# Decay exponents of sixteen attention units as a TensorE product, narrower products for Y, and a new order of the first 850 steps

## The chip, the cores and the metric

One core of a Trainium2 chip runs the kernel. The metric is device time in microseconds, taken over whole executions; one further execution is recorded by the hardware profiler, and all rows shown come from that one. Engines: PE is TensorE, DVE is VectorE, ACT is ScalarE, POOL is GpSimd, and SP issues transfers.

## The reference

An mLSTM runs over 4 x 8 heads (B x H) of 768 steps with head size 40, and its output passes through two pairs of dense layers (320 to 2048 to 320):

```python
for t in range(S):
    m_new = np.maximum(f_gate[:, :, t] + m, i_gate[:, :, t])
    f_stab = np.exp(f_gate[:, :, t] + m - m_new)
    i_stab = np.exp(i_gate[:, :, t] - m_new)
    C = f_stab[...] * C + i_stab[...] * np.einsum('bhd,bhe->bhde', vt, kt)
    n = f_stab[...] * n + i_stab[...] * kt
    y[:, :, t] = sigmoid(o_gate) * (C @ qt) / np.maximum(np.abs(n @ qt), 1.0)
h = x @ w_in;  x = (h * np.clip(h + 3.0, 0.0, 6.0) / 6.0) @ w_out     # phase 0
h = x @ w_in2; x = np.maximum(h, 0.0) ** 2 @ w_out2                   # phase 1
```

## The kernel before

**Attention.** The sequence is cut into 12 chunks of 64 steps. A *unit* u is one batch b and one chunk c with all eight heads, so there are 48. For each unit the kernel builds W = exp(G[l] + bT[j]), the decay between a row j and a step l, with G a running sum of gate values and bT a value per row, and rows after the step masked. W has 104 partitions: 64 rows of the chunk and 40 rows (from partition 64, `E0`) for the state carried from the chunk before. The steps of one unit, with their functions: `at_load` (q, k and v; L275), `at_gload` (G read back from DRAM and broadcast to 104 partitions; L287), `w_add` (adds bT; L295), `w_mask` (on POOL; L304), `w_e` (Exp on ACT; L310), `x_q` (q times W for the state rows; L326), `x_k` (k times W's last column; L333), `at_S` (the products of k and q on PE; L355), `at_P` (those times W, on DVE; L384), `at_Y` (the products with v and the state, on PE; L398), `at_C` (the new state), `at_n1` to `at_n3` (the normalization; L415 to L444). For eight units (value "p" in the table `ENG`, L174) `x_q` does nothing: `at_S` passes q through PSUM by a product with an identity (L366), and one `at_P` covers all 104 rows. Units from 22 on (`US`) round q and k to fp32r first (`qk_split`, L346).

**at_Y.** For each head there are two fp32 products: 64 output rows (L404) and 40 output rows (L406). An fp32 product is two records in the trace, so a unit has 32.

**Dense layers.** X is kept as six blocks of 128 steps by four batches. `t_pe`, `t_hi` and `t_lo` (L520 to L539) transpose a block and split it into two fp32r parts. A *slot* s is one block and 128 of the 2048 hidden columns: `mm_A` (eight products, L545), `act1` (ACT, L556), `act1b` (DVE, L564), `act2` (a rounded copy, L572), `act2b` (what is left of it, on DVE, L577), and `mm_B` (three products for each 128 rows, L582). There are 200 slots; the first 16 are of half width (256 columns), the rest of 512. Slots 0 to 23 are block 0, and phase 1 begins with slot 104. Weights come as 64-bit numbers and are decoded by `w_exp` (ACT), `w_b1` and `w_b2` (DVE), `w_hi` (ACT) and `w_lo` (mostly POOL), L484 to L513.

**Order.** Every engine runs its instructions in the order of one list of steps. The first part is written out by hand (`FIRST`, L31 to L101, 704 steps up to slot 30 and unit 21); the rest comes from `moe()` (L649), which places attention steps, transposes and weight steps at slots by hooks (L670 to L703). All transfers are issued by SP. PSUM has eight banks: four accumulators, two (`ps_a`) that `mm_A` uses in turn, one (`ps_s`) for S and transposes, one (`ps_y`) for Y.

Of the kernel before, what the change touches and what calls it, by code (L numbers as in the profile page):

```python
# [43 lines left out]
x_q:4 w_add:5 w_mask:5 w_add:7 gate_b:1 at_S:5 at_P:4,1 at_P:4,0 w_exp:0,4 w_e:6 x_q:6 w_b1:0,4
act1:0 act1:1 w_e:5 at_C:3 w_hi:0,3 x_k:5 w_lo:0,3 x_k:6 w_mask:7 x_q:5 act1b:0 mm_A:2 at_Y:4
act1b:1 w_b2:0,4 at_P:5,0 act2:0 act2:1 w_exp:0,5 act2b:0 at_P:5,1 at_n1:4 at_S:6
mm_A:3 w_b1:0,5 at_n2:4 w_load:0,8 at_load:7 at_P:6,1 w_b2:0,5 act2b:1 w_hi:0,4 act1:2
act1b:2 w_exp:0,6 at_C:4 act1:3 w_e:7 at_n3:4 w_hi:0,5 act2:2 w_lo:0,4 x_k:7 x_q:7 gate_bT:1
at_P:6,0 mm_B:0,1 at_Y:5 at_n1:5 w_b1:0,6 at_gload:8 at_load:8 w_lo:0,5 act2b:2 w_b2:0,6
w_exp:0,7 w_b1:0,7 act1b:3 at_S:7 mm_A:4 at_C:5 w_exp:0,8 at_n2:5 mm_B:1,1 mm_B:2,1  # L50
act1:4 at_P:7,0 at_P:7,1 at_Y:6 w_load:0,11 w_add:8 w_mask:8 at_gload:9 w_load:0,10 w_load:0,9
at_gload:10 at_load:9 at_load:10 at_gload:11 w_b2:0,7 act1b:4 mm_B:0,0 w_hi:0,6 at_C:6 act2:3
w_e:8 at_n1:6 at_S:8 at_P:8,1 mm_B:1,0 w_exp:0,9 w_exp:0,10 w_add:9 w_lo:0,6 w_mask:9
w_e:9 at_n2:6 w_load:0,14 warm o_load:3 load_gates:1 at_P:8,0 at_n3:6 x_k:8 at_n3:5 mm_B:2,0
at_Y:7 w_b1:0,8 act2b:3 at_n1:7 act2:4 act2b:4 w_b2:0,8 w_hi:0,7 t_pe:0,0,2 t_hi:0,0,2
# [721 lines left out]
```

## Time and profile before

| what | value |
|---|---|
| median of 3 runs | 871.29 us (871.28 to 873.6) |
| the profiled execution | 871.86 us |
| span in its profile | 870.1 us, 15963 instructions |
| mean granted TensorE clock | 0.99 of full speed |

The span runs from the first to the last instruction of the program; 1.76 us of the profiled execution lie around it. Busy times come from records: those of PE are pipelined and their ends are modelled, so distances between starts are the better measure there. Idle time in front of an instruction is put down to the event that ended it.

### The profile page before, as it was taken

The page shows a single profiled execution, that of the slowest core. Times are in us where ns is not written, and L with a number is a line of the kernel's source. Part 1 is how long each engine was busy: PE and PEld are TensorE (multiplying, and loading weights), DVE is VectorE, ACT ScalarE, POOL GpSimd, SP SyncE. Part 2 cuts the span into 40 slices and gives each one's busy share as a digit, 9 for nine tenths or more (in the row PEclk, how much of TensorE's full clock was granted, in tenths as well). Part 3 has the DMA queues.
Part 4 walks back from the last instruction along what each step waited for, and adds up shares of the span by engine and source line. Part 5 has one row for each costly group of instructions (what it writes and reads, how often), then busy time and mean ns, then how long its engine had stood idle before and what let it go on. Part 6 is the DMA issues. An engine that isn't in the chain of part 4 may idle for free.

```text
span 870.1 us, 15963 instructions
## 1 busy us (share of the span) xinstructions
PE 825.9 (95%) x6288; PEld 738.0 (85%) x6288; DVE 559.5 (64%) x938; ACT 427.4 (49%) x817; POOL 260.7 (30%) x240
## 2 busy tenths in 40 slices
...
GB/s 222 269 232 134 169 81 36 92 100 96 170 92 97 103 86 108 95 81 82 1 3 167 201 163 1 1 31 1 1 31 1 20 12 1 31 1 1 31 1 31
DMA packets 30694, 66.82 MB, mean 77 GB/s; under 512 B 5116, under 2 KB 17468, under 8 KB 30620
## 3 DMA queue, kind: packets, MB, share of 16 engines
...
q14 instruction: 25, 0.20, 0.1%
...
## 4 chain that ended last, share of the span: by engine, by line
PE 73%; DVE 16%; issue 5%; ACT 3%; POOL 1%; DMA 1%; SPq 0%; DVEq 0%; POOLq 0%; ACTq 0%
PE hps L551 33%; PE acc L590 32%; DVE wt L492 4%; DVE gl L580 3%; PE Yp L404 3%; PE Sp L372 2%; DVE g L567 2%; PE tp L525 2%; DVE wt L498 1%; DVE X L444 1%; ACT yt L431 1%; ACT g L560 1%; DVE gh L575 1%; DVE Xm L395 1%; PE Sp L379 1%
## 5 line engine op out<-in xcount | busy, mean ns | idle before, releaser
L551 PE MATMUL hps<-xs,wi 128*128 128x512 f32 (+1 forms) x1600 | 392.6, 389 | 4.2 <-DVE g L567 2.4
L590 PE MATMUL acc<-wo,gh 128*128 128x320 f32 x1536 | 349.5, 314 | 0.3 <-ACT X L597 0.3
L551 PEld LDWEIGHTS hps<-xs,wi 128*128 128x128 f32 x1600 | 290.5, 193 | 53.5 <-DVE g L567 2.7
L590 PEld LDWEIGHTS acc<-wo,gh 128*128 128x128 f32 x1536 | 259.6, 189 | 9.9 <-ACT X L597 0.5
L590 PE MATMUL acc<-wo,gl 128*128 128x320 f32 x768 | 239.3, 312 | 5.0 <-DVE gl L580 5.0
L580 DVE TENSOR_TENSOR gl<-g,gh 128x512 fp32r<-128x512 f32 (+1 forms) x200 | 154.2, 771 | 61.7 <-ACT gh L575 60.6
L575 ACT CAST gh<-g 128x512 fp32r<-128x512 f32 (+1 forms) x192 | 115.1, 600 | 75.3 <-DVE g L570 58.7
L570 DVE TENSOR_TENSOR g<-g 128x512 f32<-128x512 f32 x96 | 66.4, 692 | 133.2 <-ACT g L562 133.2
L590 PEld LDWEIGHTS acc<-wo,gl 128*128 128x128 f32 x768 | 144.9, 189 | 7.6 <-DVE gl L580 7.5
L560 ACT ACTIVATE g<-hps,three 128x512 f32<-128x512 f32 (+1 forms) x104 | 67.8, 655 | 152.0 <-PE hps L551 138.4
L562 ACT ACTIVATE g<-hps 128x512 f32<-128x512 f32 x96 | 57.3, 597 | 143.4 <-PE hps L551 143.4
L567 DVE SCALAR_TENSOR_TENSOR g<-g,hps 128x512 f32<-128x512 f32 (+1 forms) x104 | 66.8, 644 | 65.0 <-ACT g L560 64.5
L329 POOL TENSOR_TENSOR Xm<-qkt,W 40x512 f32<-40x512 f32 x36 | 49.8, 1384 | 119.2 <-ACT W L319 113.6
L404 PEld LDWEIGHTS Yp<-Z,Xm 104*64 104x64 f32 x768 | 54.5, 151 | 21.8 <-issue 13.3
L404 PE MATMUL Yp<-Z,Xm 104*64 104x41 f32 x768 | 60.6, 244 | 8.8 <-DVE Xm L388 3.8
L300 POOL TENSOR_TENSOR W<-W,bT 104x512 f32<-104x512 f32 x43 | 59.4, 1382 | 3.4 <-DMA W<-Gd 3.0
L406 PE MATMUL Yp<-Z,Xm 104*40 104x41 f32 x768 | 52.7, 225 | 0.3 <-POOL Xm L340 0.3
L512 POOL TENSOR_TENSOR wi<-wt,wi 128x768 fp32r<-128x768 f32 x14 | 27.6, 1970 | 83.7 <-ACT wi L507 83.5
L340 POOL TENSOR_TENSOR Xm<-kI,W 104x320 f32<-104x320 f32 x43 | 40.5, 944 | 25.2 <-DMA Z<-in_va 10.4
L406 PEld LDWEIGHTS Yp<-Z,Xm 104*40 104x40 f32 x768 | 46.5, 123 | 0.4 <-POOL Xm L340 0.4
L351 DVE SCALAR_TENSOR_TENSOR qs<-qs,less,qkt 120x512 fp32r<-120x512 f32 x52 | 37.6, 764 | 7.5 <-ACT qs L349 7.3
L306 POOL TENSOR_SCALAR_AFFINE_SELECT W<-W 64x512 f32<-64x512 f32 x48 | 36.7, 767 | 9.7 <-DVE W L300 6.8
...
## 6 DMA issues: line engine op xcount, KB each, us to landing
...
W<-Gd SPq DMA_DIRECT2D x48, 208.0 KB
...
```

The costliest lines, as they stand in the source:

```text
L300: on("w_add", "g", u).tensor_tensor(out=W, in0=W, in1=bT[:, c, b * H:(b + 1) * H].unsqueeze(2).to_broadcast([KX, H, L]), op=ALU.add)
L329: on("x_q", "g", u).tensor_tensor(out=x_tile(u)[E0:KX, :, 0:L], in0=T["qk", u][E0:KX, 0], in1=T["W", u][E0:KX], op=ALU.mult)
L404: nc.tensor.matmul(out=Yp[0:L, h, :], lhsT=Xm[:, h, 0:L], rhs=Z[b][c % 2][:, h, :], start=True, stop=True)
L406: nc.tensor.matmul(out=Yp[E0:KX, h, :], lhsT=Xm[:, h, L:KX], rhs=Z[b][c % 2][:, h, :], start=True, stop=True)
L551: nc.tensor.matmul(out=h, lhsT=w[:, hl, kk, o:o + P], rhs=t[:, xk, i0 * P:i1 * P], start=(i == 0), stop=(i == len(TERMS) - 1))
L560: nc.scalar.activation(out=g, in_=T["h", s], func=ACTF.Relu, bias=three)
L562: nc.scalar.activation(out=g, in_=T["h", s], func=ACTF.Relu)
L567: nc.vector.scalar_tensor_tensor(out=g, in0=g, scalar=6.0, in1=T["h", s], op0=ALU.min, op1=ALU.mult)
L570: nc.vector.tensor_tensor(out=g, in0=g, in1=g, op=ALU.mult)
L575: copy("act2", s)(out=gh, in_=g)
L580: nc.vector.tensor_tensor(out=gl, in0=g, in1=gh.bitcast(F32), op=ALU.subtract)
L590: nc.tensor.matmul(out=acc[i], lhsT=g[:, n], rhs=w[:, hl, m % MG, :], start=(m == 0 and q == 0), stop=(m == NM - 1 and q == 2))
```

## The change

- For the first 16 units (`U1`) W's exponent is made on PE (`w_pe`): one bf16 product of an identity with a mask, then one fp32r product of `gb` (the row values bT as a rounded part and its remainder, and two rows of ones) with `R[b]` (rows that select the heads, and two rows that hold G's rounded part and remainder). `w_e` reads the sum from PSUM. `w_add` and `w_mask` are left out for these units. G goes to `R[b]` by two small transfers inside the core, issued by ACT, not by a broadcast from DRAM. The bank is that of an accumulator for units 0 to 7, and `ps_s` for 8 to 15.
- The same 16 units send q through PSUM in `at_S` (eight did so before).
- In all units `at_Y` computes each head in four products with at most 32 output rows (32, 32, 32, 8), where there were two.
- In slots 0 to 23 `act1b` writes g over h in its PSUM bank, so that `act2` and `act2b` read PSUM.
- The constants are made in five smaller steps, with eight ACT copies for the head rows (`head_rows`); two gate steps move from POOL to DVE.
- The written list is new: 845 steps, up to slot 40 and unit 26. A mark "@v", "@g" or "@a" names the engine in place of the table `ENG`. Before `mm_A:30` both lists have the steps of 30 slots, all 16 weight tiles of phase 0 and `at_Y` of 20 units.
- Phase 1's weight decoding starts a tile every one and a half slots, where it was every slot.

```diff
@@ -29,75 +30,86 @@
 FIRST = """
-o_load:1 load_gates:0 o_load:0 o_sig:0 o_sig:1 at_load:0 at_load:1 const_init gate_m:0 gate_g:0
-gate_G:0 gate_b:0 gate_bT:0 gate_m:1 gate_g:1 at_load:2 at_gload:0 at_gload:1 w_load:0,0
-at_gload:2 at_gload:3 w_add:0 w_mask:0 w_e:0 x_q:0 w_add:1 w_mask:1 at_S:0 at_S:1 at_S:2
...
-t_pe:0,0,0 at_C:2 w_add:6 t_hi:0,0,0 t_lo:0,0,0 warm at_n3:3 w_exp:0,3 t_pe:0,0,1 warm w_hi:0,2
-t_hi:0,0,1 w_b1:0,3 w_b2:0,3 t_lo:0,0,1 w_lo:0,2 mm_A:0 at_S:4 mm_A:1 x_k:4 w_mask:6
...
+const_g load_gates:0 const_z:0 const_i at_load:0 head_rows:1 at_load:1 const_z:1 head_rows:0
+const_l const_z:3 const_z:2 head_rows:2 gate_m:0 o_load:0 const_k:1 at_load:2 gate_g:0 head_rows:3
+at_S:0 gate_G:0 w_load:0,0 gate_b:0 at_gload:0 at_gload:4 at_gload:1 const_k:2 gate_bT:0 at_S:1
+at_gload:5 const_k:0 w_load:0,2 gate_m:1 gate_g:1 w_pe:0 gate_G:1 o_sig:0 w_pe:1 gate_b:1 w_e:0
+w_load:0,1 w_e:1 at_P:0,0 x_k:0 at_gload:2 at_P:1,0 at_gload:3 gate_bT:1 at_Y:0 x_k:1@v at_S:2
...
+t_lo:0,0,1 w_exp:0,3 w_lo:0,2@v mm_A:0 w_load:0,7 w_b2:0,1 mm_A:1 act1:0 w_b1:0,4 w_hi:0,1 at_S:4
...
+at_P:5,0 at_Y:4 w_exp:0,5 at_load:8 w_lo:0,4 act1b:3 mm_B:0,0 act2:2 at_n1:4 at_S:6 at_C:4 act2b:2
+load_gates:1 act2:3 at_n2:4 x_k:6 w_exp:0,7 mm_A:4 at_P:6,0 at_load:9 w_b1:0,6 mm_B:1,0 act1:4
+at_Y:5 w_b2:0,6 mm_B:1,1 w_load:0,10 at_n1:5 at_C:5 at_S:7 w_hi:0,6 x_k:7@v act2b:3 w_exp:0,8
...
 """
@@ -187,6 +192,14 @@
     cuts = [0, 2, 4, NC]
     SE = cuts[2] * L
     gt = wpool.tile([P, 2 * KI3 * GC], F32, tag=f"wi{NG - 1}", name="gt")[0:BH]
+
+    Gp = wpool.tile([P, 2, NC1 * L], F32R, tag=f"wo{NG - 1}", name="Gp")[0:BH]
+
+
+    KW = 2 * BH + 2
+    pre = xs_p.tile([P, 5, TB], F32R, tag="xs", name="pre")
+    R = [pre[0:KW, b] for b in range(B)]
+    gb = pre[0:KW, B, 0:NC1 * KX].rearrange("p (c k) -> p c k", k=KX)
     gx, gy = (t[0:BH].rearrange("p b d -> p (b d)") for t in X[NPR - 2:])
     def gate_views(r):
@@ -210,23 +223,43 @@
         nc.sync.dma_start(out=f0, in_=gates[:, 0, a:z])
         nc.sync.dma_start(out=i0, in_=gates[:, 1, a:z])
-    def const_init():
+    def const_g():
         nc.vector.memset(gate_views(0)[2][:, 0:1], -1e30)
         ones_but_first(rst)
+
+    def const_i():
+        make_identity(nc, ident)
+        nc.scalar.copy(out=identb, in_=ident[0:L, 0:KX])
+        nc.vector.memset(gb[0:2 * BH].bitcast(F32), 0.0)
+        nc.vector.memset(gb[2 * BH:KW].bitcast(F32), 1.0)
+        nc.gpsimd.memset(maskb, 0.0)
+        nc.gpsimd.affine_select(
+            out=maskb, in_=maskb, pattern=[[0, H], [1, L]], compare_op=ALU.is_ge,
+            fill=-1e30, base=0, channel_multiplier=-1)
+
...
+    def head_rows(b):
+        for i in range(2):
+            r = slice(BH * i, BH * i + BH)
+            nc.scalar.copy(
+                out=R[b][r].rearrange("p (h l) -> p h l", l=L),
+                in_=ident[r, BH * i + b * H:BH * i + (b + 1) * H].unsqueeze(2).to_broadcast(
+                    [BH, H, L]))
     def gate_m(r):
         f, i, m, _ = gate_views(r)
@@ -253,6 +286,11 @@
             ones_but_first(d)
         nc.vector.tensor_tensor_scan(
             out=G, data0=d, data1=G, initial=0.0, op0=ALU.mult, op1=ALU.add)
+        if r < 2:
+            hi, lo = (Gp[:, i, c0 * L:c1 * L] for i in range(2))
+            nc.vector.tensor_copy(out=hi, in_=G)
+            nc.vector.tensor_tensor(out=lo, in0=G, in1=hi.bitcast(F32), op=ALU.subtract)
+            return
         nc.sync.dma_start(
             out=Gd[c0:c1].rearrange("c h l -> h c l"), in_=G.rearrange("h (c l) -> h c l", l=L))
@@ -264,10 +302,16 @@
     def gate_bT(r):
         c0, c1 = cuts[r], cuts[r + 1]
+        if r < 2:
+            b = gate_views(r)[1].rearrange("h (c l) -> h c l", l=L)
+            hi, lo = (gb[BH * i:BH * i + BH, c0:c1, 0:L] for i in range(2))
+            nc.scalar.copy(out=hi, in_=b)
+            nc.vector.tensor_tensor(out=lo, in0=b, in1=hi.bitcast(F32), op=ALU.subtract)
+            return
@@ -286,11 +330,29 @@
     def at_gload(u):
         b, c = units[u]
-        W = at2.tile([KX, H, L], F32, tag="W", name="W", bufs=4)
+        if u < U1:
+            for i in range(2):
+                nc.scalar.dma_start(
+                    out=R[b][2 * BH + i:2 * BH + i + 1].bitcast(F32),
+                    in_=Gp[b * H:(b + 1) * H, i, c * L:(c + 1) * L].bitcast(F32))
+            return
+        W = w_tile(u)
         nc.sync.dma_start(
             out=W,
             in_=Gd[c, b * H:(b + 1) * H].rearrange("h l -> (h l)").partition_broadcast(KX))
-        T["W", u] = W
+
+    def w_tile(u):
+        T["W", u] = at2.tile([KX, H, L], F32, tag="W", name="W", bufs=4)
+        return T["W", u]
+
+    def w_pe(u):
+        b, c = units[u]
+        pool, tag = (ps_acc, f"acc{2 + u % 2}") if u < 8 else (ps_s, "s")
+        w_tile(u)
+        Wp = T["Wp", u] = pool.tile([KX, TB], F32, tag=tag, name="Wp")
+        nc.tensor.matmul(
+            out=Wp, lhsT=identb, rhs=maskb.rearrange("p h l -> p (h l)"), start=True, stop=False)
+        nc.tensor.matmul(out=Wp, lhsT=gb[:, c], rhs=R[b], start=False, stop=True)
     def w_add(u):
         b, c = units[u]
@@ -309,12 +371,16 @@
     def w_e(u):
         b, c = units[u]
+        if u < U1:
+            nc.scalar.activation(
+                out=T["W", u], in_=T["Wp", u].rearrange("p (h l) -> p h l", l=L), func=ACTF.Exp)
+            return
@@ -324,7 +390,7 @@
         return T["X", u]
     def x_q(u):
-        if ENG.get(("x_q", u)) == "p":
+        if u < U1:
             return
         on("x_q", "g", u).tensor_tensor(
             out=x_tile(u)[E0:KX, :, 0:L], in0=T["qk", u][E0:KX, 0], in1=T["W", u][E0:KX],
@@ -383,7 +450,7 @@
     def at_P(u, o):
         W, Xm, Sp = T["W", u], x_tile(u), T["S", u]
-        if ENG.get(("x_q", u)) == "p":
+        if u < U1:
             if o == 0:
                 nc.vector.tensor_tensor(out=Xm[:, :, 0:L], in0=Sp[0:KX], in1=W, op=ALU.mult)
             return
@@ -401,10 +468,11 @@
         pool, tag = (ps_acc, "acc0") if u in (1, 3) else (ps_y, "y")
         Yp = pool.tile([KX, H, DV], F32, tag=tag, name="Yp")
         for h in range(H):
-            nc.tensor.matmul(
-                out=Yp[0:L, h, :], lhsT=Xm[:, h, 0:L], rhs=Z[b][c % 2][:, h, :], start=True, stop=True)
-            nc.tensor.matmul(
-                out=Yp[E0:KX, h, :], lhsT=Xm[:, h, L:KX], rhs=Z[b][c % 2][:, h, :], start=True, stop=True)
+            for o in range(0, KX, 32):
+                e = min(o + 32, KX)
+                nc.tensor.matmul(
+                    out=Yp[o:e, h, :], lhsT=Xm[:, h, o:e], rhs=Z[b][c % 2][:, h, :],
+                    start=True, stop=True)
         T["Y", u] = Yp
     def at_C(u):
@@ -562,12 +630,14 @@
             nc.scalar.activation(out=g, in_=T["h", s], func=ACTF.Relu)
     def act1b(s):
-        g = T["g", s] = T["r", s]
+        r = T["r", s]
+
+        g = T["g", s] = T["h", s] if s < GP else r
         if slots[s][0] == 0:
             nc.vector.scalar_tensor_tensor(
-                out=g, in0=g, scalar=6.0, in1=T["h", s], op0=ALU.min, op1=ALU.mult)
+                out=g, in0=r, scalar=6.0, in1=T["h", s], op0=ALU.min, op1=ALU.mult)
         else:
-            nc.vector.tensor_tensor(out=g, in0=g, in1=g, op=ALU.mult)
+            nc.vector.tensor_tensor(out=g, in0=r, in1=r, op=ALU.mult)
     def act2(s):
         g = T["g", s]
@@ -693,24 +763,27 @@
         for i in range(B):
             at(first[1, j, 0] - 13 + 3 * i, "pe", x_T, 1, j, i)
     s1 = first[0, NB - 1, 0] + 2
+
+
     for i in range(NS):
         at(s1 + i, "ew", w_load, 1, i)
-        at(s1 + i + 3, "ew", w_exp, 1, i)
-        at(s1 + i + 4, "ew", w_bits, 1, i)
-        at(s1 + i + 5, "ew", w_hilo, 1, i)
+        s = s1 + 3 + 3 * i // 2
+        at(s, "ew", w_exp, 1, i)
+        at(s + 1, "ew", w_bits, 1, i)
+        at(s + 2, "ew", w_hilo, 1, i)
```

## Rows read from the trace of the kernel before

**Rows 1.** The page, busy time of each engine, with its share of the span.
```profile
PE 825.9 (95%) x6288; PEld 738.0 (85%) x6288; DVE 559.5 (64%) x938; ACT 427.4 (49%) x817; POOL 260.7 (30%) x240
```
**Rows 2.** Windows: stretch, length, busy PE, PEld, DVE, ACT, POOL; clock, DMA, GB/s.
```profile
0.00:42.02 42.02, 17.64 (x243) 15.10 (x243) 27.02 (x52) 21.89 (x53) 26.31 (x42) 1.00 0.88 246
42.02:140.00 97.98, 84.98 (x941) 75.20 (x940) 85.81 (x143) 61.69 (x165) 71.27 (x61) 0.91 0.48 146
140.00:186.02 46.02, 45.29 (x445) 40.23 (x444) 34.49 (x70) 27.06 (x65) 17.70 (x18) 1.00 0.22 63
186.02:515.86 329.84, 328.40 (x2703) 292.10 (x2701) 251.17 (x434) 177.67 (x290) 133.87 (x115) 1.00 0.38 104
515.86:540.19 24.33, 23.60 (x128) 20.14 (x127) 24.00 (x29) 15.86 (x29) 11.10 (x7) 1.00 0.08 28
540.19:870.10 329.91, 326.02 (x1840) 295.23 (x1838) 136.97 (x215) 123.19 (x220) 0.42 (x1) 1.00 0.04 13
```
**Rows 3.** Windows of L551 (`mm_A`) alone: length, busy PE (count), busy PEld (count).
```profile
42.02:186.02 144.00, 52.36 (x240) 42.25 (x241) 0.94 0.40 119
515.86:540.19 24.33, 12.02 (x48) 8.75 (x49) 1.00 0.08 28
830.19:858.93 28.74, 16.00 (x64) 11.68 (x65) 1.00 0.00 1
```
**Rows 4.** Timeline of PE around one unit: start, length, what.
```profile
366.04 2.00 PE L551 MATMUL hps<-xs,wi 128*128 128x512 f32 x8
...
369.97 2.00 PE L551 MATMUL hps<-xs,wi 128*128 128x512 f32 x8
371.90 0.25 PE L404 MATMUL Yp<-Z,Xm 104*64 104x41 f32 x1
...
372.21 0.23 PE L404 MATMUL Yp<-Z,Xm 104*64 104x41 f32 x1
372.22 0.21 PE L406 MATMUL Yp<-Z,Xm 104*40 104x41 f32 x1
372.27 0.23 PE L404 MATMUL Yp<-Z,Xm 104*64 104x41 f32 x1
...
372.96 0.65 PE L372 MATMUL Sp<-qs 120*64 120x64 f32 x8
```
**Rows 5.** Timeline of PE, the 40-row products at the start of another Y.
```profile
189.25 0.20 PE L406 MATMUL Yp<-Z,Xm 104*40 104x41 f32 x1
...
189.29 0.24 PE L406 MATMUL Yp<-Z,Xm 104*40 104x41 f32 x2
...
189.37 0.20 PE L406 MATMUL Yp<-Z,Xm 104*40 104x41 f32 x1
```
**Rows 6.** Timeline of PE, S with q through PSUM, to the following Y.
```profile
95.50 0.27 PE L364 MATMUL Sp<-qkt 40*64 40x64 f32 x1
...
96.57 0.25 PE L404 MATMUL Yp<-Z,Xm 104*64 104x41 f32 x1
```
**Rows 7.** Groups by line and shape, DVE: count, busy us, mean ns.
```profile
L444 DVE TENSOR_TENSOR X<-X,yt 64x320 f32<-64x320 f32 x34 | 35.4, 1042 | 1.1
...
L580 DVE TENSOR_TENSOR gl<-g,gh 128x256 fp32r<-128x256 f32 x16 | 19.9, 1247 | 0.4 <-ACT gh L575 0.4
...
L567 DVE SCALAR_TENSOR_TENSOR g<-g,hps 128x256 f32<-128x256 f32 x16 | 6.5, 412 | 4.6 <-ACT g L560 4.5
```
**Rows 8.** L580 alone: shortest, median and longest, in ns.
```profile
L580 DVE TENSOR_TENSOR gl<-g,gh x200: 365/693/2869, 51.9 to 863.0; 128x512 fp32r<-128x512 f32 x92, 128x256 fp32r<-128x256 f32 x8
```
**Rows 9.** Groups by line and shape, POOL: count, busy us, mean ns.
```profile
L300 POOL TENSOR_TENSOR W<-W,bT 104x512 f32<-104x512 f32 x43 | 59.4, 1382 | 3.4 <-DMA W<-Gd 3.0
...
L306 POOL TENSOR_SCALAR_AFFINE_SELECT W<-W 64x512 f32<-64x512 f32 x48 | 36.7, 767 | 9.7 <-DVE W L300 6.8
```
**Rows 10.** The page, DMA issues: count, KB each.
```profile
W<-Gd SPq DMA_DIRECT2D x48, 208.0 KB
```
**Rows 11.** Timeline of SP's queue: start of two issues and their time together.
```profile
11.83 0.74 SPq L290 DMA_DIRECT2D W<-Gd  x2
```

More of the change, by code (lines that the diff above doesn't have):

```diff
@@ L10 @@
 F32R = mybir.dt.float32r
+BF16 = mybir.dt.bfloat16
 I32 = mybir.dt.int32
@@ L44 @@
[L44 to L55, printed above, removed]
@@ new lines @@
+load_gates:1 act2:3 at_n2:4 x_k:6 w_exp:0,7 mm_A:4 at_P:6,0 at_load:9 w_b1:0,6 mm_B:1,0 act1:4
+at_Y:5 w_b2:0,6 mm_B:1,1 w_load:0,10 at_n1:5 at_C:5 at_S:7 w_hi:0,6 x_k:7@v act2b:3 w_exp:0,8
+w_lo:0,6 at_load:10 at_P:7,0 mm_A:5 act1b:4 w_pe:8 at_n2:5 act2:4 w_load:0,9 act1:5 act2b:4 at_Y:6
+w_e:8 act1b:5 mm_A:6 w_b2:0,3 at_gload:12 at_C:6 at_n1:6 w_hi:0,3 at_S:8 w_load:0,12 at_n3:4 act1:6
+at_n2:6 w_lo:0,3 x_k:8@a act1b:6 at_Y:7 at_P:8,0 at_n3:6@g at_n1:7 mm_B:2,0 mm_B:2,1 at_C:7@v
+at_load:11 mm_B:3,1 w_exp:0,10 w_b1:0,5 t_pe:0,0,2 w_b2:0,5 mm_B:3,0 t_hi:0,0,2 at_n3:5 act2:5
@@ new lines @@
+act1:10 mm_B:8,2 act1:11 act1b:10 at_n3:8@g mm_B:9,2 act1b:11 act2:10 mm_B:9,3 act2b:10 w_pe:10
+w_exp:0,14 gate_G:2 mm_A:12 w_e:10 mm_B:10,3 act1:12 mm_B:10,2 at_gload:14 act2:11@v at_S:9 x_k:9
+o_sig:2 act2b:11 act1b:12 mm_A:13 at_P:9,0 at_load:12 act2:12 act2b:12 mm_B:11,2 act1:13 w_b1:0,10
+at_S:10 o_sig:3 act1b:13 x_k:10 mm_A:14 at_P:10,0 act2:13 at_load:13 act2b:13 mm_B:12,2 act1:14
+mm_B:11,3 w_b2:0,10 mm_A:15 act1b:14 w_hi:0,10 gate_b:2 w_pe:11 act2:14 mm_B:12,3 w_e:11 at_Y:9
+act2b:14 w_lo:0,10 o_load:5 act1:15 w_pe:12 at_gload:15 act1b:15 at_C:9 mm_A:16 at_n1:9 act2:15
```

183 lines of the change are left out of this document (91 added, 92 removed).

## The prediction

> **What bounds the kernel now.** I read the busy shares first, then the windows by stage, then the starts on PE. PE is busy 95% of the span, and no other engine over 64% [rows 1]. The windows show that this is an average over different stages [rows 2]. Up to 42.02 us, where the first mm_A starts, PE has little to do, and the DMA engines are 88% busy at 246 GB/s. From 42 to 140 us DVE is busy 85.8 of 98.0 us and POOL 71.3, and the granted clock is only 0.91, so this stage is bound by the elementwise engines. From 140 us PE is busy nearly all the time, with one exception: from 515.86 to 540.19 us, where phase 1's weights are decoded, DVE is busy 24.00 of 24.33 us. The 240 products of L551 between 42.02 and 186.02 us are 30 slots [rows 3], so mm_A:30 starts at 186.02. Both lists reach that step with 20 units through at_Y; I compare there.
>
> In the last stretch eight slots take 28.74 us, 3.59 each [rows 3]. A slot with a transposed group takes 3.93 (366.04 to 369.97) [rows 4]. What lies behind 186 us and is not on PE is hidden, and what leaves PE there leaves the time.
>
> **Y in narrower products.** One unit's Y takes 1.06 us on PE now (371.90 to 372.96), 32 records. A 64-row record and the 40-row record of the other output half start 0.01 us apart, and the next pair 0.06 us after the first [rows 4]. So the two run beside each other, and a round of two costs what the wider one costs. Where the 40-row products run ahead of the wide ones, their own starts are 0.04 us apart (189.25, .29, twice in the merged row, and .37) [rows 5]. Narrower is faster, then, and records for different output rows don't wait for each other. The change makes rounds of four, none over 32 rows. I take 0.04 us a round, the nearest row: 16 x 0.04, and the 0.10 that is left of 1.06 after 16 x 0.06, is 0.74, so 0.32 less per unit. The bounds: four starts 0.01 apart in a round give 0.04 as well, and half of that overlap would still be 0.03 (Y 0.58, 0.48 less); if every record keeps the 0.033 us that it has now (1.06 / 32), 64 records cost 2.12, which is 1.06 more. After mm_A:30 28 units are left in both lists: 28 x 0.32 = **9.0 us less** (from 13.4 less to 29.7 more).
>
> This is where a rule speaks against the change. The Trainium skill (TensorEngine Tiling (Array Packing), Instruction Overhead) says that a product of one column costs as much as one of 60, about 60 cycles, and that one should not tile a dimension that is small already; TensorE: Matmul & The Clock Gate (Back-to-back issue gap) puts a floor of about 25 ns between starts. By that, an estimate, 64 records are 1.6 us, 0.6 more per unit. The starts 0.01 us apart in rows 4 don't show this floor between records for different output rows.
>
> **Up to the first mm_A, 42 us.** 246 GB/s for 42.02 us is 10.3 MB. The new list moves less before mm_A:0: eight broadcasts of W, 1.7 MB [rows 10], one weight tile and one block of o_gate less, some 3 MB or 12 us at that rate. Five masks (0.77 us) and three adds (1.38) leave POOL [rows 9]. Against that ACT gets eight copies of 512 elements and 24 transfers to issue; two issues take SP 0.74 us [rows 11], so about 9 us on ACT if it pays the same, on top of 21.9 busy [rows 2]. That fits into 42 us, but not far below. Bounds 0 and 12 us less; I take **5 less**, nearer to nothing since ACT fills up.
>
> **From mm_A:0 to mm_A:30, 144 us.** I counted the steps of both lists between these two marks, by engine.
> - DVE: before, 85.8 + 34.5 = 120.3 us [rows 2]. The new order gives it eight more at_n2, six more at_n3 (1.04 [rows 7]), three more weight steps, and takes five copies and some x_q away: 4.8 more in sum. What leaves it is a stretch: act2b at half width takes 1247 ns in the mean and 365 at best [rows 7, 8], while act1b of the same size, which reads h in PSUM, takes 412. All operands of act2b lie in SBUF now; with g in PSUM I take 412 for it: 16 x 0.835 = 13.4 less. Sum 111.7.
> - POOL: fourteen adds go to eight, seventeen masks to seven, and some x_q and at_n3 leave. That is 71.3 + 17.7 down to about 50. at_n3 and the weight steps on DVE are all in SBUF too; if POOL's share is what stretches them, up to 12 us more leave DVE. No row parts this cleanly, so the bounds are 0 and 12.
> - PE: 14 full slots at 3.59, 16 half ones at about 1.8, 17 S, each with q through PSUM at most 1.07 (95.50 to 96.57) [rows 6], 16 Y at 0.74, eight w_pe of two 512-column products (2.00 / 8 = 0.25 us each at most [rows 4]) and six transposes at 0.34: 50 + 29 + 18 + 12 + 4 + 2 = 115. Of this, w_pe and S with q are new work that the stage's idle PE covers; if it became PE-bound they would cost some 8 us.
> - ACT: 61.7 + 27.1 before; it loses nine at_n2 pieces and gains about 4 us of issues. Not the bound.
>
> At DVE's present share (85.8 of 98.0) 111.7 us give 128, 16 less; with all of POOL's relief 114, 30 less, where PE's 115 stops it. I take **20 less**, nearer to the end that needs no relief.
>
> **New waits.** An issue of at_gload on ACT waits for gate_G, or for the w_pe that last read the same rows of R; w_exp, act1 and w_e stand behind it on ACT, and PE waits for the landing at w_pe. mm_A(s + 2) waits for act2b(s) now, not act1b(s): act1, act1b, act2 and act2b of a half slot are some 1.7 us, and a half slot is 1.8 us of PE, with two banks in turn: hidden while DVE isn't late. From unit 8 w_pe shares the one S bank with S and the transposes, each held until Exp or at_P has read it; the other banks' products cover this only as the order places it. If that cover is gone it is part of the second rival.
>
> **Phase 1's weights.** Six slots take 24.33 us [rows 3]; at 3.59 each, and with two transposes at 0.34, they would take 22.2. A third of a tile less per slot leaves DVE under PE: **2.1 less** (0 to 2.1).
>
> **Sum.** The new list has four mm_B groups fewer before mm_A:30, 1.6 us to pay later at about 0.4 ((28.74 - 16.00) / 32 [rows 3]). So 870.1 - 5 - 20 - 9.0 - 2.1 + 1.6 = 835.6 us of span; with the 1.76 around it 837.4, against 871.86 for the profiled execution, which lies 0.57 above the median. I predict **837 us**, about 4% less.
>
> **Rivals.**
> - *Every narrow record keeps its own turn on PE* (the other side). Place: at_Y of all units. Y costs 2.12: 29.7 more over the last 28 units, and 22 more for PE in the stage before, whose 115 becomes 137, so nothing is gained there. 870.1 - 5 - 2.1 + 1.6 + 29.7 + 1.8 = 896. It decides from about 0.105 us a round of four. For it: no row shows a product under 40 rows. Against it: the starts 0.01 apart. Chance 0.09. By the skill's floor it would be milder: about 875, an estimate.
> - *The early order doesn't hold.* Place: ACT's queue, where an issue that waits holds up Exp and the weight steps, and the S bank. The first 186 us stay what they are: 870.1 - 9.0 - 2.1 + 1.6 + 1.8 = 862. For it: the list is timed to the step, and nothing in the trace shows an issue on ACT. Against it: DVE, the busiest engine there, loses work whatever the order. Chance 0.13.
> - *The narrow products change nothing*, since a round is held by something other than its width: 837 + 9 = 846 (a little more in the stage before). Chance 0.04.
>
> **How the numbers follow.** The forecast has 0.74; the bounds of its terms reach from 819 (30, 12 and 13.4 less, not all at once) to about 852. A tenth above that belongs to the second rival, so the range is 819 to 862; some 5% lie under it and 13% over it. About 0.3% is what a measurement here can tell from no change, 868.7 to 873.9: faster 0.87 (the forecast, the third rival and nearly all of the second), same 0.04 (between the first two rivals), slower 0.09.
>
> **What would show it.** Starts of L404's successor in rounds of about 0.04 us and a Y of 0.7 us between 186 and 480; act2b of half slots near 0.4 us; POOL under 60% between 42 and 140; mm_A:30 starting near 161 us; slots of 3.59 us where the weights are decoded. A Y over 1.06 us makes the prediction wrong in its sign; an mm_A:30 near 186 puts it at the second rival.

## The result: 858.5 us, the direction right and less than half of the gain

The changed kernel takes 858.52 us (median of 4 runs, 857.28 to 859.85) against 872.44 for the kernel before beside it: ratio 0.9839, 95% interval 0.9814 to 0.9864, so 1.6% less. I had said 837 us, 4% less, and 819 to 862 as the range. The time lies in the range, near its upper end.

The profiled execution has a span of 856.8 us. The page's line of busy shares is the first thing to set beside [rows 1]:

```profile
PE 820.4 (96%) x7968; PEld 724.2 (85%) x7968; DVE 534.0 (62%) x963; ACT 415.5 (48%) x727; POOL 205.8 (24%) x188
```

POOL lost 55 us of work and DVE 25, but PE only 5.5, and PE is what bounds most of the span. The windows, cut as in [rows 2], show where the time went. mm_A:0 is at 46.60 and mm_A:30 at 178.50. The six slots at the decode of phase 1's weights are mm_A:105 to mm_A:111 here and mm_A:106 to mm_A:112 there. The columns are those of [rows 2]:

```profile
0.00:46.60 46.60, 24.87 (x407) 16.09 (x407) 23.50 (x67) 21.12 (x34) 6.73 (x20) 1.00 0.59 191
46.60:140.00 93.40, 87.54 (x1400) 75.14 (x1401) 71.87 (x149) 58.77 (x112) 38.32 (x33) 0.95 0.47 147
140.00:178.50 38.50, 37.64 (x593) 32.59 (x592) 30.27 (x62) 19.34 (x40) 22.00 (x21) 1.00 0.33 93
178.50:501.60 323.10, 318.55 (x3590) 281.75 (x3589) 242.03 (x440) 170.99 (x288) 120.63 (x106) 1.00 0.35 98
501.60:523.90 22.30, 22.30 (x129) 20.18 (x128) 17.64 (x24) 14.98 (x27) 7.28 (x5) 1.00 0.17 62
523.90:856.80 332.90, 329.53 (x1859) 298.40 (x1858) 148.66 (x226) 130.32 (x230) 10.88 (x6) 1.00 0.04 13
```

| stretch | before | after | difference | forecast |
|---|---|---|---|---|
| start to mm_A:0 | 42.0 | 46.6 | +4.6 | -5 |
| mm_A:0 to mm_A:30 | 144.0 | 131.9 | -12.1 | -20 |
| mm_A:30 to the end | 684.1 | 678.3 | -5.8 | -9.5 |

All three terms fell short, the first with the wrong sign. My signs of a right step are there, but for one: mm_A:30 was to start near 161 us, and starts at 178.50. POOL's share between 46.6 and 140 is 41% (38.32 of 93.40; before, 71.27 of 97.98). Y takes 0.73 us, in the timeline of PE against [rows 4], from its start to that of the mm_B behind it; its sixteen rounds of four records start 0.04 us apart in the mean:

```profile
221.26 0.80 PE L473 MATMUL Yp<-Z,Xm 104*32 104x41 f32 x64
221.99 0.56 PE L660 MATMUL acc<-wo,gh 128*128 128x320 f32 x2
```

act2b of half slots is down to 413 ns from 1247, beside act1b of the same size (groups by line and shape, against [rows 7]):

```profile
L637 DVE SCALAR_TENSOR_TENSOR hps<-g,hps 128x256 f32<-128x256 f32 x16 | 6.7, 424 | 5.1 <-ACT g L628 5.0
L650 DVE TENSOR_TENSOR gl<-hps,gh 128x256 fp32r<-128x256 f32 x16 | 6.5, 413 | 0.9 <-ACT gh L645 0.3
```

**Where the start went.** ACT's timeline (ACTq are the transfers that it issues; "x5" merges five) has the fault in it:

```profile
6.55 1.45 ACTq L335 DMA_DIRECT2D pre<-Gp  x1
6.61 0.62 ACT L259 CAST pre<-ident 32x512 fp32r<-32x512 f32 x1
8.10 8.24 ACTq L335 DMA_DIRECT2D pre<-Gp  x5
16.38 0.30 ACT L308 CAST pre<-gt 32x128 fp32r<-32x128 f32 x1 [9.15 <-DMA pre<-Gp]
...
21.60 1.08 ACT L375 ACTIVATE W<-Wp 104x512 f32<-104x512 f32 x2
...
34.25 7.25 ACTq L335 DMA_DIRECT2D pre<-Gp  x6
41.60 0.76 ACT L481 COPY Z<-Yp 40x328 f32<-40x328 f32 x2 [7.05 <-DMA pre<-Gp]
```

Six issues of at_gload hold ACT's queue from 6.55 to 16.34 us, with gate_bT (L308) and then the first Exp (L375) behind them. Six more hold it from 34.25 to 41.50, with at_C:2 (L481), and so the rest of unit 2, behind them. One issue takes 0.63 us; the line's own view gives the shortest, the median and the longest in ns, and who waited:

```profile
L335 ACTq DMA_DIRECT2D pre<-Gp x32: 627/627/1452, 6.5 to 105.0; - x32
...
  ACT pre L308: 9.1, 1
  ACT Z L481: 7.1, 1
```

Six times 0.63 is 3.8 us, and the first stall is 9.8. The chain of work shows what the rest is:

```profile
7.91 7.77 DMA rwi<-in_w1i
15.69 0.02 issue
15.71 0.63 ACTq L335
16.33 0.04 issue
16.38 0.30 ACT pre L308
```

A small issue on ACT waits there until a weight tile that SP asked for at 7.91 us has landed. The listing of the built program's instructions says why. In this program eight DMA semaphores serve all transfers in turn, and a transfer waits until the one that had its semaphore before has landed. Here SP's second weight load and ACT's sixth transfer of at_gload have the same one:

```
SP  L542 DMA rwi1_230<-in_w1i 128x768      [waits DMAHW5_49]
ACT L335 DMA pre_119<-Gp_118 1x8x64        [waits DMAHW5_49]
```

So a 2 KB transfer whose data is ready waits, on ACT, for a 768 KB one. In the second stall the chain runs through another weight load, asked for at 31.25 us:

```profile
31.25 4.86 DMA rwo<-in_w1o
36.10 0.02 issue
36.12 0.02 ACTq L335
```

Before the change no transfer was issued on ACT, and only SP's other transfers stood behind such a wait.

### The profile page after: what moved, and what is told of

The parts are those of the page before. It is cut to its first block, busy times and chain, and to the rows that moved or that the text cites. A ratio compares the mean times of both kernels' runs of the same rounds, so it can differ in the third digit from the quotient of the medians.

```text
span 856.8 us, 19209 instructions
## 1 busy us (share of the span) xinstructions
PE 820.4 (96%) x7968; PEld 724.2 (85%) x7968; DVE 534.0 (62%) x963; ACT 415.5 (48%) x727; POOL 205.8 (24%) x188
## 4 chain that ended last, share of the span: by engine, by line
PE 83%; DVE 5%; DMA 4%; ACT 4%; issue 2%; SPq 2%; ACTq 0%; POOL 0%; POOLq 0%; DVEq 0%
PE hps L619 38%; PE acc L660 36%; PE Yp L473 3%; PE tp L595 2%; PE Sp L439 2%; DMA qkt<-in_qk 1%; DVE qs L417 1%; DMA rwi<-in_w1i 1%; ACT qs L415 1%; PE Sp L431 1%; PE Sp L433 1%; DMA rwo<-in_w1o 1%; DVE X L512 1%; DMA pre<-Gp 0%; DVE Xm L455 0%
## 5 line engine op out<-in xcount | busy, mean ns | idle before, releaser
L650 DVE TENSOR_TENSOR gl<-g,gh 128x512 fp32r<-128x512 f32 x176 | 128.2, 730 | 65.9 <-ACT gh L645 64.9
L645 ACT CAST gh<-g 128x512 fp32r<-128x512 f32 x168 | 104.1, 619 | 67.5 <-DVE g L640 53.3
L637 DVE SCALAR_TENSOR_TENSOR g<-g,hps 128x512 f32<-128x512 f32 x80 | 54.8, 686 | 53.3 <-ACT g L628 53.0
L395 POOL TENSOR_TENSOR Xm<-qkt,W 40x512 f32<-40x512 f32 x29 | 38.3, 1321 | 111.8 <-ACT W L385 77.4
L580 POOL TENSOR_TENSOR wi<-wt,wi 128x768 fp32r<-128x768 f32 x15 | 29.7, 1979 | 128.5 <-ACT wi L575 125.5
L473 PEld LDWEIGHTS Yp<-Z,Xm 104*32 104x32 f32 (+1 forms) x3072 | 35.0, 109 | 20.4 <-issue 12.4
L473 PE MATMUL Yp<-Z,Xm 104*32 104x41 f32 (+1 forms) x3072 | 41.1, 208 | 6.9 <-DVE Xm L455 4.6
L362 POOL TENSOR_TENSOR W<-W,bT 104x512 f32<-104x512 f32 x32 | 44.3, 1386 | 1.5 <-DMA W<-Gd 1.4
L580 POOL TENSOR_TENSOR wo<-wt,wo 128x640 fp32r<-128x640 f32 x16 | 26.0, 1626 | 49.0 <-ACT wo L575 46.4
L512 DVE TENSOR_TENSOR X<-X,yt 64x320 f32<-64x320 f32 x39 | 32.6, 836 | 1.1
L481 ACT COPY Z<-Yp 40x328 f32<-40x328 f32 x41 | 17.4, 427 | 30.5 <-PE Yp L473 11.1
```

Source lines behind the costliest of these rows:

```text
L362: on("w_add", "g", u).tensor_tensor(out=W, in0=W, in1=bT[:, c - NC1, b * H:(b + 1) * H].unsqueeze(2).to_broadcast([KX, H, L]), op=ALU.add)
L473: nc.tensor.matmul(out=Yp[o:e, h, :], lhsT=Xm[:, h, o:e], rhs=Z[b][c % 2][:, h, :], start=True, stop=True)
L580: on("w_lo", "g", ph, i).tensor_tensor(out=w[:, 1], in0=f, in1=w[:, 0].bitcast(F32), op=ALU.subtract)
L637: nc.vector.scalar_tensor_tensor(out=g, in0=r, scalar=6.0, in1=T["h", s], op0=ALU.min, op1=ALU.mult)
L645: copy("act2", s)(out=gh, in_=g)
L650: nc.vector.tensor_tensor(out=gl, in0=g, in1=gh.bitcast(F32), op=ALU.subtract)
```

## The experiments

Twelve kernels. Spans and starts are of the profiled executions, the medians of the timed ones; they are each compared with the kernel before on the same chip, which had medians of 871.8 to 872.3 us.

| kernel | median us | first Exp | mm_A:0 | to mm_A:30 | from there |
|---|---|---|---|---|---|
| changed | 858.5 | 21.6 | 46.6 | 131.9 | 678.3 |
| late_w (the same program) | 857.8 | 21.8 | 48.0 | 128.6 | 679.8 |
| y_only | 861.3 | 17.3 | 42.3 | 139.7 | 676.6 |
| wide_y | 867.9 | 21.6 | 48.2 | 134.1 | 684.1 |
| gp0 | 856.7 | 22.0 | 47.2 | 127.5 | 680.4 |
| gload_sp | 848.1 | 14.5 | 38.7 | 127.7 | 679.8 |
| pair | 848.5 | 17.1 | 39.8 | 128.3 | 678.8 |
| late_89 | 858.1 | 22.5 | 46.2 | 131.5 | 678.8 |
| late_act | 862.7 | 16.5 | 41.8 | 141.3 | 677.8 |
| cut30 | 853.1 | 21.5 | 46.7 | 129.0 | 674.7 |
| sp_pair | 845.7 | 14.9 | 36.5 | 129.9 | 679.0 |
| sp_pair_cut | 840.1 | 15.1 | 36.6 | 126.4 | 674.8 |
| sp_pair_cut_gp0 | 840.8 | 15.2 | 37.6 | 126.3 | 674.6 |

**late_w: a miss that became a repeat.** w_load:0,0 and w_load:0,2 were moved in the list:

```diff
-at_S:0 gate_G:0 w_load:0,0 gate_b:0 at_gload:0 at_gload:4 at_gload:1 ... at_gload:5 const_k:0 w_load:0,2
+at_S:0 gate_G:0 gate_b:0 at_gload:0 at_gload:4 at_gload:1 ... at_gload:5 w_load:0,0 w_load:0,2 const_k:0
```

> The changed kernel with the first two weight loads (w_load:0,0 and 0,2) moved from ahead of at_gload:0 and behind at_gload:5 to behind at_gload:5, both. Theory: each issue waits for the transfer that held its DMA semaphore before (eight semaphores for all queues); the fifth and sixth issue of at_gload (14.43 and 15.71 us) waited for exactly these two loads. They then wait for nothing late: the sixth issue ends at 13 to 14.5 instead of 16.33 us, the first Exp comes at 18.5 to 20 instead of 21.6, and mm_A:0 1.5 to 3 us earlier; total 855 to 857.5. Rival: the issues are held by the load on the DMA engines (the q, k, v and gate loads still stand ahead), no change: 858 to 860; or the weights' own delay costs more than it gives, 860 to 863.

Measured: 857.77 us (ratio 0.9835, 0.9796 to 0.9874), first Exp at 21.77. Neither theory was tried. The loads stand in SP's queue and at_gload in ACT's, and on neither queue did any instruction change its place or its wait: the built program is the same. I should have seen that a list over several queues has orders that mean nothing. What it gives is a repeat: two profiles of one program differ by 3.3 us between mm_A:0 and mm_A:30 (the granted clock was below full speed for longer in the first) and by 1.5 behind it. Differences of that size in the table are not read.

**Issues off ACT (gload_sp), and half as many on ACT (pair).**

```diff
-                nc.scalar.dma_start(
+                nc.sync.dma_start(
```

> The changed kernel with at_gload's 32 small transfers issued by SyncE instead of ScalarE, order kept. Theory: the start is late because ScalarE stands 9.8 us in six of these issues (0.63 us each, and waits for earlier transfers in between) with gate_bT and the first Exp behind them, and again from 34.3 to 41.5 us with at_C:2 behind them. Off ScalarE, the first Exp comes at about 17 to 18 instead of 21.6 us and mm_A:0 at 38 to 43 instead of 46.6; total 850 to 855. SyncE's loads wait a little for them. Rival: the start is late through the order of the list and the TensorE route, or the same waits simply move to SyncE and the loads behind it: mm_A:0 stays at 46 to 48, total 857 to 860.

```diff
+            if b % 2:
+                return
             for i in range(2):
                 nc.scalar.dma_start(
-                    out=R[b][2 * BH + i:2 * BH + i + 1].bitcast(F32),
-                    in_=Gp[b * H:(b + 1) * H, i, c * L:(c + 1) * L].bitcast(F32))
+                    out=pre[2 * BH + i:2 * BH + i + 1, b:b + 2].bitcast(F32),
+                    in_=Gp[b * H:(b + 2) * H, i, c * L:(c + 1) * L].bitcast(F32))
```

> The changed kernel with one at_gload for two batches (the rows of b and b+1 in one transfer of 4 KB each for hi and lo): 16 issues on ScalarE instead of 32, at the place of the later of the two steps (the first two pairs at the earlier). Theory: the price is per issue and per wait for an earlier transfer, so the first Exp comes 2 to 4 us earlier (18 to 19.5) and the stall at 34 to 41 us halves; mm_A:0 at 40 to 44, total 852 to 856. Rival as in the run with SyncE: mm_A:0 unchanged, 857 to 860.

Measured: 848.06 us with SP (ratio 0.9731, 0.9707 to 0.9756) and 848.51 with pairs (0.9735, 0.9714 to 0.9755), both some 10 us better than the changed kernel and better than I had expected. On SP, ACT's timeline has nothing ahead of gate_bT, and Exp comes 7 us earlier:

```profile
7.25 0.30 ACT L308 CAST pre<-gt 32x128 fp32r<-32x128 f32 x1
...
14.45 0.60 ACT L375 ACTIVATE W<-Wp 104x512 f32<-104x512 f32 x1 [1.10 <-PE Wp L355]
```

The same view with pairs, where four issues stand ahead (L229 is gate_bT, L298 Exp):

```profile
6.79 6.06 ACTq L258 DMA_DIRECT2D pre<-Gp  x4
12.95 0.30 ACT L229 CAST pre<-gt 32x128 fp32r<-32x128 f32 x1 [5.72 <-DMA Z<-in_va]
...
17.14 0.60 ACT L298 ACTIVATE W<-Wp 104x512 f32<-104x512 f32 x1
```

mm_A:0 is 7.9 and 6.8 us earlier and the gain stays to the end. The rival, that the order of the list or the route through PE makes the start late, falls: both are unchanged in gload_sp. An issue costs SP the same (median 632 ns), but behind it there stand only loads that are wanted later.

**Order alone, on ACT (late_89, late_act).**

```diff
-at_gload:7 at_gload:6 at_gload:8 at_P:3,0 at_gload:9 at_C:2
+at_gload:7 at_gload:6 at_P:3,0 at_C:2
...
-mm_A:3
+mm_A:3 at_gload:8 at_gload:9
```

> The changed kernel with at_gload:8 and at_gload:9 (four issues on ScalarE) moved from behind at_gload:6 to behind mm_A:3; they are needed only by w_pe:8 and 9. Theory: the second stall of ScalarE (34.25 to 41.5 us, with at_C:2 behind it) is on the path to mm_A:0 and half of it or more goes: mm_A:0 at 41 to 44 instead of 46.6 us, the first Exp unchanged at 21.6; total 853 to 856. Rival: the path to mm_A:0 is set by the first stall alone or by the weights, mm_A:0 unchanged, 857 to 860.

Measured: 858.06 us (0.9834, 0.9805 to 0.9862), mm_A:0 at 46.2. at_C:2 came 3.8 us earlier, as it should, and the next issues, at_gload:11 and 10, took the place of the stall:

```profile
35.26 2.44 ACTq L256 DMA_DIRECT2D pre<-Gp  x2
37.80 0.43 ACT L402 COPY Z<-Yp 40x328 f32<-40x328 f32 x1 [2.38 <-DMA pre<-Gp]
...
42.55 3.05 ACTq L256 DMA_DIRECT2D pre<-Gp  x4
45.64 0.48 ACT L520 CAST xs<-tp 128x384 fp32r<-128x384 f32 x1 [2.57 <-DMA pre<-Gp]
```

L520 is t_hi:0,0,1, the copy that mm_A:0 waits for. So my number was wrong, and not because the stall was off the path: there was another behind it. late_act moves these two as well, and at_gload:4 and 5 out of the first stall:

```diff
-at_gload:0 at_gload:4 at_gload:1 ... at_gload:5 ... w_e:1
+at_gload:0 at_gload:1 ... w_e:1 at_gload:4 at_gload:5
...
-mm_A:3
+mm_A:3 at_gload:8 at_gload:9 at_gload:11 at_gload:10
```

> The changed kernel, issues kept on ScalarE and all 32 of them, order alone changed: at_gload:4 and 5 behind w_e:1, at_gload:8, 9, 11 and 10 behind mm_A:3. Theory: what counts is which issues stand ahead of gate_bT and of the copies on ScalarE, and which earlier transfer each must wait for. The four issues left at the start hold no semaphore of a weight load, end at about 12.4 us instead of 16.33 (with the fifth and sixth, 17.7), so the first Exp comes at 16.5 to 18 instead of 21.6; of the second stall only at_gload:7 and 6 are left. mm_A:0 at 39 to 43 instead of 46.6; total 850 to 855. Rival: ScalarE's issues are slow there whatever their place, because the DMA engines are loaded with the q, k, v, gate and weight loads; then the four still end near 16 us, mm_A:0 at 45 to 48, total 856 to 860.

Measured: 862.67 us (0.9897, 0.9866 to 0.9928). The start did what the theory says, nearly to the digit: four issues ended at 12.22, Exp came at 16.46, mm_A:0 at 41.8. So ACT's issues are not slow there as such; it is which transfer they wait for. But the total is worse than both theories had it, because the issues moved behind mm_A:3 hold ACT there:

```profile
47.56 10.61 ACTq L256 DMA_DIRECT2D pre<-Gp  x7
58.27 0.47 ACT L549 ACTIVATE g<-hps,three 128x256 f32<-128x256 f32 x1 [10.24 <-DMA pre<-Gp]
```

L549 is act1 of a slot. The act1b behind it waits 9.2 us for it on DVE, an at_P stands behind that on DVE's queue, and PE waits 7.4 us for the at_P. A window of this kernel over that stretch has PE at 7.08 busy of 14.50 us, with a mean granted clock of 0.83:

```profile
47.20:61.70 14.50, 7.08 (x150) 6.30 (x150) 5.00 (x12) 4.21 (x10) 2.53 (x3) 0.83 0.41 112
```

In each of the three orders tried on ACT (the changed kernel's, late_89's and late_act's) something that is wanted stands behind the issues. An order that spreads them out singly was not tried.

**Narrow Y alone, and everything else without it (y_only, wide_y).** y_only is the kernel before with the new at_Y:

```diff
-            nc.tensor.matmul(
-                out=Yp[0:L, h, :], lhsT=Xm[:, h, 0:L], rhs=Z[b][c % 2][:, h, :], start=True, stop=True)
-            nc.tensor.matmul(
-                out=Yp[E0:KX, h, :], lhsT=Xm[:, h, L:KX], rhs=Z[b][c % 2][:, h, :], start=True, stop=True)
+            for o in range(0, KX, 32):
+                e = min(o + 32, KX)
+                nc.tensor.matmul(
+                    out=Yp[o:e, h, :], lhsT=Xm[:, h, o:e], rhs=Z[b][c % 2][:, h, :],
+                    start=True, stop=True)
```

> The kernel before with one edit: at_Y issues its products in column groups of 32 and 8 as the changed kernel does (64 records for 32). Theory: the narrow Y is a term of its own that acts where TensorE is the bound, so 28 units after mm_A:30 at 0.32 us each, about -9 us: 872.4 becomes 863 (861 to 865), Y at about 0.73 us a unit, and the time from mm_A:0 to mm_A:30 stays at 144 us because VectorE bounds it. Rival 1: Y is off the path everywhere, 872. Rival 2: Y was on the path in the early stage too, then 5 to 6 us more, 857, and the rest of the change (product route, banks, new order) brought nothing at all.

wide_y takes the same edit out of the changed kernel.

> The changed kernel with at_Y's two products per head as before (64 and 40 rows) instead of four of 32, 32, 32 and 8. Theory: TensorE is the bound from mm_A:0 on in the changed kernel, so all units count: 0.32 us in 28 units behind mm_A:30 (-9 of the forecast) and 0.35 us or more in 16 units in the stage before it, 11 to 16 us slower than the changed kernel: 869.5 to 874.5, which leaves next to nothing of the gain. Rival: the gain of narrow Y is the same as in the kernel before (10.8 us) or less, because waits at at_S take its place: 865 to 869.3.

Measured: y_only 861.3 us (0.9883, 0.9856 to 0.9909), 10.8 less than before; wide_y 867.94 (0.9962, 0.9946 to 0.9979), 9.4 more than the changed kernel. So of the 13.9 us that the whole change gained, narrow Y gives about 10, and the product route, the banks and the new order together 3 to 4.5. In y_only, PE's busy time behind mm_A:30 falls from 678.0 (the last three of [rows 2]) to 668.93, by 9.1 or 28 x 0.325, and the stretch by 7.5:

```profile
182.00:858.60 676.60, 668.93 (x5561) 598.32 (x5560) 407.70 (x676) 316.67 (x536) 146.03 (x121) 1.00 0.21 58
```

Its other 4.3 us lie before mm_A:30, where I had expected none; that is little more than the spread of the repeat. For wide_y my theory fell, and the time is in the rival's range: behind mm_A:30 the changed kernel has 8.6 us less of PE work than wide_y (670.4 and 678.9 us busy), but is only 5.8 us shorter. Whether the new order takes the rest is the next run.

**The order behind mm_A:30 (cut30).** The written list ends at mm_A:30, and the loop's own order, with its default engines, goes on from there.

```diff
-mm_A:30 at_P:20,0
-at_gload:24 x_k:21@v qk_split:23 ... act2:39@v act2b:39
+mm_A:30
```

> The changed kernel whose written-out order ends at mm_A:30, with the order of the loop (default engines too) from there on. Theory: of the narrow Y's gain 2.4 us were given back behind mm_A:30 by waits that the new order makes there (at_S 0.8 to 1.4 us late for Xm and qs); the run of the kernel before with narrow Y alone took 676.6 us from mm_A:30 to the end, this one 678.3. With the default order the stretch from mm_A:30 to the end takes 675.5 to 677.5, total 855.5 to 857.5. Rival: the new order is worth what it says there and the default one is no better on it: 678 to 682, total 858 to 862.

Measured: 853.07 us (0.9787, 0.9757 to 0.9817), 5.4 less than the changed kernel, and 674.7 us from mm_A:30 to the end, a little better than I had put it. Of the 5.4 us, 3.6 lie in that stretch. The table bears it out: the three kernels with the loop's order there take 674.6 to 674.8 us for it, the eight with narrow Y and the written order 677.8 to 680.4. The waits of PE between mm_A:30 and mm_A:50, first in the changed kernel, then here (us in total, times, longest):

```profile
PE Sp L439 <- DVE Xm L462: 1.4, 1, 1.4
PE Sp L439 <- DVE qs L417: 1.2, 2, 0.8
PE Yp L473 <- POOL X L512: 0.4, 1, 0.4
PE hps L619 <- DVE rd L486: 0.3, 1, 0.3
PE Sp L439 <- DVE xs L606: 0.2, 1, 0.2
```

```profile
PE Sp L360 <- DVE qs L338: 1.2, 2, 0.8
```

The written order has an S wait 1.4 us for the at_P that reads the bank before it, and three small waits more, on top of the one that the loop's order has too. That is 2.3 of the 3.6 us; where the rest goes is not shown.

**The PSUM bank (gp0).**

```diff
-    GP = 24
+    GP = 0
```

> The changed kernel with GP = 0: g goes back to its SBUF tile in the first 24 slots, all else stays. Theory: TensorE bounds the stage mm_A:0 to mm_A:30 now (87.5 of 93.4 us busy from 46.6 to 140, VectorE 71.9), so act2b getting slower (413 ns to some 600 to 1000, GpSimd is busy 41% there) is mostly taken by VectorE's slack: mm_A:30 from 178.5 to 179 to 184, total 859 to 864. Rival: VectorE is still what ends the stage, then 24 slots (18 of them half slots) times 0.3 to 0.8 us all show, 866 to 878, and the stage's gain came from the bank.

Measured: 856.73 us (0.9823, 0.9798 to 0.9847), the same as the changed kernel or a little less. act2b of half slots, in the groups by line and shape:

```profile
L650 DVE TENSOR_TENSOR gl<-g,gh 128x256 fp32r<-128x256 f32 x16 | 9.4, 598 | 1.9 <-ACT gh L645 1.4
```

Of the 834 ns that it lost (1247 to 413) only 185 are missing without the bank; the other 649 come with g in SBUF too. The timelines show why. The same decode step of POOL runs beside an act2b of half width in both kernels, first with g in SBUF (gp0), then with g in PSUM (the changed kernel):

```profile
78.66 1.57 POOL L580 TENSOR_TENSOR wo<-wt,wo 128x640 fp32r<-128x640 f32 x1 [4.01 <-ACT wo L575]
79.44 1.08 DVE L650 TENSOR_TENSOR gl<-g,gh 128x256 fp32r<-128x256 f32 x1
```

```profile
80.83 1.59 POOL L580 TENSOR_TENSOR wo<-wt,wo 128x640 fp32r<-128x640 f32 x1 [5.32 <-ACT wo L575]
81.06 0.43 DVE L650 TENSOR_TENSOR gl<-hps,gh 128x256 fp32r<-128x256 f32 x1
```

With g in SBUF act2b ends 0.28 us behind the end of POOL's step. All four half-width ones that take over 600 ns in gp0 began while POOL was at work and do so (0.27 to 0.29 us behind), and so do all ten in the kernel before (0.28 to 0.35); the nine in gp0 with no POOL record beside them take 405 to 427. With g in PSUM POOL records lie beside eight of the sixteen, and none takes over 426. So by these records either step helps by itself: the bank frees act2b from POOL, and less work on POOL leaves little to be freed from. The kernel before with the bank alone was not run. In the changed kernel the bank's 16 x 0.185 = 3 us of DVE don't show in the time, since DVE doesn't bound the stage any more.

**Both repairs (sp_pair, sp_pair_cut, sp_pair_cut_gp0).** sp_pair joins the edits of gload_sp and pair, sp_pair_cut adds cut30's, and the last has GP = 0 as well.

> Both earlier edits together: rows of two batches in one transfer, issued by SyncE. Theory: ScalarE has no issue in its way (as with SyncE alone, mm_A:0 at 38.7) and SyncE has half as many, so its loads behind the issues come earlier as well: mm_A:0 at 36 to 38.5, total 844 to 848. Rival: the start is set by something else by now (the weights' decode or TensorE's stretch of 2.4 us at 20.3), mm_A:0 at 38.5 to 40, total 847 to 850.

> The repair of the start (rows of two batches in one transfer, issued by SyncE) and the default order behind mm_A:30 together. Theory: the two faults are at different places and add: mm_A:0 at 36 to 38 us, 128 to 130 us to mm_A:30, 674.5 to 676.5 us from there; total 840 to 844. Rival: an earlier start only moves the wait (weights and loads later, the stage's gain eaten before mm_A:30), or the default order is worth less behind this stage: 845 to 849.

> The same with GP = 0 (g back in its SBUF tile). Theory from the earlier run with GP = 0: TensorE bounds the stage and act2b's extra 0.2 us in each half slot fits into VectorE's slack, so nothing: within 2 us of the kernel beside it. Rival: with the start mended VectorE has less slack and the bank is worth 3 to 6 us.

Measured: 845.68 (0.9694, 0.9666 to 0.9721), then 840.1 (0.9655, 0.9622 to 0.9689) and 840.75 us (0.9647, 0.9617 to 0.9677). The faults add, and the bank is worth nothing here either. The windows of sp_pair_cut, from the start to mm_A:0, to mm_A:30 and to the end:

```profile
0.00:36.60 36.60, 24.92 (x407) 16.11 (x407) 23.52 (x67) 21.53 (x34) 6.72 (x20) 1.00 0.69 211
36.60:163.00 126.40, 119.78 (x1991) 102.71 (x1991) 102.75 (x210) 78.05 (x151) 61.20 (x54) 0.99 0.48 147
163.00:837.80 674.80, 668.83 (x5574) 599.86 (x5572) 401.35 (x678) 316.86 (x536) 141.40 (x117) 1.00 0.19 55
```

This is faster than both kernels, 3.5% below the one before. With both repairs the stretches come near what I had forecast for the changed kernel: 37.0, 124 and 674.6 us, 835.6 of span, against 36.6, 126.4, 674.8 and 837.8.

## Why the prediction was right in direction and wrong in size

**Narrow Y: right.** 0.74 us was forecast and 0.73 measured, the rounds start 0.04 us apart as forecast, and 9.1 us leave PE behind mm_A:30. Both rivals that denied this, the records that keep their own turn and the products that change nothing, are out. So is the rule that I weighed: 64 records in 0.73 us are 11 ns apart. By the Trainium skill's floor of about 25 ns between starts (TensorE: Matmul & The Clock Gate, Back-to-back issue gap) they would, by estimate, take 1.6 us, and its advice not to tile a small dimension (TensorEngine Tiling (Array Packing), Instruction Overhead) would have spoken for leaving Y alone. For products into different output rows the measurement decides against both.

**Start to mm_A:0: the step that failed.** It read: "two issues take SP 0.74 us, so about 9 us on ACT if it pays the same", and that this "fits into 42 us". Two things were wrong. The price was that of another transfer; this one costs 0.63 us to issue on either queue, so 24 cost 15 us. And I counted the issues as work to be added up, where they are places in a queue. I had named what an at_gload waits for (gate_G, or the w_pe before), and not the landing of an earlier transfer with the same semaphore, SP's weight loads among them. The eight semaphores can be read from the program before; I looked at the queues one by one and took them for independent. gload_sp and sp_pair show that these issues are the miss: with them off ACT mm_A:0 starts at 38.7 us, which is 7.9 of the 9.6 us, and with half as many of them at 36.5, where the forecast had 37.0. The Trainium skill (DMA: Bandwidth & Descriptors, Issuing engines are not separate DMA queues) says that issuing from several engines saves only the sequencer's time, usually small beside the transfer. Here that time was the larger matter: the same 32 issues moved from ACT to SP took 10.4 us off the total (858.5 to 848.1). An issue costs the same on both; on ACT wanted work stood behind it.

**mm_A:0 to mm_A:30: the way was right, the floor on PE too low, 4 to 8 us short.** DVE did leave the bound (71.87 of 93.40 us from 46.6 to 140, 85.81 of 97.98 before), and PE took its place. I had put the 124 us between 128 for DVE and 115 for PE, and neither of these held. DVE has 102.1 us of work there in the changed kernel (71.87 and 30.27), where I had 111.7, and POOL 60.3 for my 50. The term that was mis-sized is PE's sum of 115. It measures 120 (119.78 in sp_pair_cut). By distances between starts there, the products of the slots make 84 us of it for my 79 and w_pe 5.5 for my 4, while S is some 2 less. On top come 6 to 9 us of waits, for which the sum had nothing. So it is in part luck that 126.4 lies so near 124. In the profile of the changed kernel a mean granted clock of 0.95 from 46.6 to 140 goes with some 3 us more (131.9, and 128.6 in the repeat, which has 0.98 there). The reason given for act2b, "with g in PSUM I take 412 for it", was right in its number. But most of this gain did not need the bank: gp0 shows that POOL's relief, the effect that I had set at 0 to 12 us because no row parted the two, gives 649 of the 834 ns by itself. The Trainium skill (SBUF — State Buffer, SBUF: two separate sides) has a rule for this: an operation of DVE with two inputs in SBUF and one of POOL that reads SBUF exclude each other. The trace agrees: 1247 ns with POOL 73% busy, 598 with it at 43%, 413 and never over 426 with one operand in PSUM.

**Behind mm_A:30: right, then partly given back.** The 22.30 us for six slots at the decode of the weights are what I had (22.2). With the loop's order (sp_pair_cut) the whole stretch loses 9.3 us, for 9.5 forecast. The written order loses 3.5 of them again; the prediction took the order behind mm_A:30 to cost nothing, without naming it.

**The second rival** had the place right: ACT's queue, "where an issue that waits holds up Exp and the weight steps". Its time, 862, was nearer than my forecast, and I gave it 0.13 with the reason that DVE loses work whatever the order. That is true of DVE and says nothing of the start, which DVE does not bound. That 862 came so near is in part luck, since the rival had the first 186 us unchanged: the start lost 4.6 us, and the stage behind it gained 12.1.

What stays open: in gload_sp PE stands still for 2.4 us in the middle of a Y at 20.33 us and waits for nothing that the profile shows; I tried nothing on it. Nor did I try what the other 2 us of sp_pair_cut's stage would take.
